# Second chunk of the first pass: Strassen's seven products in place of sixteen plain steps, with the weight sums made earlier

## Chip, core and metric

One core of one Trainium2 chip. The metric is the device time of one launch in microseconds (us), the median of several runs. The core has five engines with a queue of their own each, worked off in order: PE (TensorE, matmul), DVE (VectorE), ACT (ScalarE), POOL (GpSimd) and SP (SyncE, which here only issues DMAs). Engines wait for one another through semaphores. All data are float32.

## The reference

A retention block (attention with a decay mask and no softmax) feeds a two-layer network:

```python
# q, k, v: (8, 8, 576, 64)
scores = q @ k.T / sqrt(64)
ret    = (scores * Dmat) @ v          # Dmat[i, j] = gamma[h] ** (i - j) for i >= j, else 0
x = ret.transpose(0, 2, 1, 3).reshape(4608, 512)

# w_in: (512, 2048), w_out: (2048, 512)
h  = x @ w_in
sp = softplus(h)
g  = h * erf(sp)
out = g @ w_out                       # (4608, 512)
```

## The kernel before

**Pieces and stages.** The 8 x 576 tokens are cut into 36 pieces of 128 tokens (`pieces`). Each piece passes three stages (line 434): `transposes` (T), `scores` (S) and `outputs` (O). The text writes T8 for the transposition of piece 8, and so on. Pieces 0 to 7 have q and k transposed on PE and copied out of PSUM by ACT. From piece 8 on (`SQUARES`) q arrives in 32-column squares and is transposed on DVE (line 326), and from piece 12 on k too. S makes the score matrix on PE and multiplies it by the mask on DVE (`sT`, line 352). O multiplies by v on PE, scales the result into the token tile `x[0, c]` on DVE (two scalings, and between them a sum for the running state), multiplies the state by its decay on POOL (line 427) and emits loads for later pieces. `weigh_values` (line 313) multiplies the v of the next piece by its decay on POOL.

**Chunks and passes.** Four pieces are a chunk c of 512 tokens, so there are 9 chunks. The hidden width is cut into four groups g. A pass is one g over all chunks, and the tokens of chunk c are written to DRAM (`store_x`) in the first pass and read back (`load_x`) in the later ones. For every (g, c) there is a `First` (x times w_in, then softplus, erf, multiply) and a `Second` (times w_out). The text calls them F0, F1, F2 and S0, S1 for g = 0. S0 begins after F1.

**Strassen.** A `First` in the usual form makes seven products of 2 x 2 blocks in place of eight (`first`, `middle`, `last`). Their names are those of the weight operand: A11, A12, S2, S3, S1, S4, A22. Each is 4 matmuls, which the profile records as 8 of 128x256. They need sums of token blocks (`operands_x`, four DVE operations on 128x512 for g = 0) and sums of weight blocks (`sums_in`, four DVE operations, called "wa" in the list of a part's `sums`). `sums_in` overwrites the raw block A21 in the slot S3. The first two chunks of the first pass are `plain` instead: 16 steps of 2 matmuls (4 records) each, which read the raw blocks and the raw weights. `Second` has always seven products (B11, B21, T2, T3, T1, B22, T4) with the sums of `sums_out` ("wb").

**Weights.** They come as float64 words, and `rounding` turns them into float32. A part takes five steps: ACT (lines 254 and 255), DVE at 259, 263 and 267, and one step of DVE (272) with two POOL multiplications and additions (274 and 275; on DVE for the first four parts). `round_weights(n)` takes n steps. For g = 0 there are four parts of w_in and four of w_out.

**Order.** Nothing is scheduled by a planner: every engine works in the order in which the program emits. The start is a string of letters (line 754): `a` attends one stage, `p` is one plain step of F0, a digit is so many rounding steps, `w` loads weights. Then `attend(after_chunk(1))` brings the stages up to O7, and a loop over F1's plain steps puts one stage between every second of them, one rounding step after each, and F0's softplus, erf, multiply and sums at given steps. Then come S0's first two products, and the loop over `blocks` (line 789), in which each step of a product is followed by one stage through `attend`. Before F2 begins, all stages up to O11 are emitted and `operands_x(0, 2)` follows.

PSUM: F1 takes the banks `a` (two), `e` and `g`; stages take four banks `at`.

Of the kernel before, what the change touches and what calls it, by code (L numbers as in the profile page):

```python
# [2 lines left out]

# [1 line left out]

# [49 lines left out]
def kernel(  # L55
# [16 lines left out]
    n_dc = D_MODEL // P  # L72
    OH = D_MODEL // 2
    FH = D_FF // 2
    GP = 2
# [22 lines left out]
    def tt(out, in0, in1, op):  # L98
        nc.vector.tensor_tensor(out=out, in0=in0, in1=in1, op=op)  # L99
# [50 lines left out]
    def load(i, names="qkv"):  # L150
        if i < len(pieces):
            t = loaded.setdefault(i, {})
            for name in names:
                src = {"q": q, "k": k, "v": v}[name]
                if name == "q" and i < SQUARES:
                    t["q"] = load_rows(i, "q", q, 2)
                elif name == "q":
                    t["qs"] = load_squares(i, "q", q)
                    if i >= SQUARES_K:
                        t["ks"] = load_squares(i, "k", k)  # L160
                elif name == "v" or i < SQUARES_K or len(pieces[i]) == 1:
                    t[name] = load_rows(i, name, src, 4)
# [29 lines left out]
    def parts():  # L192

        w2 = w_in.rearrange("(e c d) (h f) -> c e d h f", c=n_dc, d=D, h=2)
        for g in range(n_g):
            for dc in range(n_dc):
                a = A11 if dc < 2 else A12
                src = [(heads[(e + dc) % 2], w2[dc, e, :, :, 2 * g * GW : 2 * (g + 1) * GW]) for e in range(2)]

                yield src, "wa", g, a, dc % 2, ["wa"] if g > 0 and dc == n_dc - 1 else []  # L200
            for f in range(2):
                for j in range(GP):
                    ft = f * FH // P + g * GP + j
                    src = [(slice(0, P), w_out[ft * P : (ft + 1) * P, :].rearrange("p (h o) -> p h o", h=2))]
                    sums = (["wb"] if g > 0 else ["wb", "wa"]) if (f, j) == (1, GP - 1) else []
                    yield src, "wb", g, B21 if f else B11, j, sums

    def sums_in(a11, s3, a12, a22, s1, s2, s4):
# [9 lines left out]
    def sums_out(b11, t3, b21, b22, t1, t2, t4):  # L218
# [7 lines left out]
        yield  # L226

    coming = parts()
    words = []
    most_g = [1]  # L230

    def load_weights():
        part = next(coming, None)
        if part is not None:
            t = wraw.tile([P, 2 * WP], UINT32, tag="wraw", name="wraw")
            for rows, src in part[0]:
                nc.sync.dma_start(out=t[rows].rearrange("p (h f) -> p h f", h=2), in_=src)
            words.append((t, *part[1:]))
# [49 lines left out]
    def round_weights(n=1):  # L288
        for _ in range(n):
            next(round_step, None)  # L290
# [149 lines left out]
    done = [0]  # L440

    def before_chunk(c):

        return stages.index((outputs, c * PC)) if c < n_ch else len(stages)

    def after_chunk(c):

        return stages.index((outputs, (c + 1) * PC - 1)) + 1

    def attend(upto):  # L450
        while done[0] < min(upto, len(stages)):
            of, i = stages[done[0]]
            of(i)
            done[0] += 1

    PLAIN = 2

    def load_x(g, c):  # L460
        x[g, c] = x_tile()
# [2 lines left out]
    def store_x(c):  # L464
        nc.sync.dma_start(out=xd[c], in_=x[0, c][:, :n_dc])
# [3 lines left out]
    def operands_x(g, c):  # L469
        summed.add((g, c))  # L470
        t = x[g, c]
        b11, b12, b21, b22 = (t[:, 2 * d : 2 * d + 2, h * TH : (h + 1) * TH] for d in range(2) for h in range(2))
        t1, t2, t4 = (t[:, n_dc + j, :].rearrange("p (d i) -> p d i", d=2) for j in range(3))
        if g == 0 or c < PLAIN:
            tt(t1, b12, b11, ALU.subtract)
            tt(t2, b22, t1, ALU.subtract)
            tt(b12, b22, b12, ALU.subtract)
        else:
            tt(t2, b12, b11, ALU.add)
            tt(t1, b22, t2, ALU.subtract)  # L480
        if g == 0:
            store_x(c)
        tt(t4, b21, t2, ALU.subtract)
        x[g, c] = {A11: b11, A12: b21, S4: b22, A22: t4, S1: t1, S2: t2, S3: b12}
# [240 lines left out]
    firsts = [First(g, c) for g, c in order]  # L725
    seconds = [Second(f) for f in firsts]
# [8 lines left out]
    def keep_busy(n):  # L735
        for _ in range(n):
            nc.tensor.matmul(idle[:, :P], lhsT=ones, rhs=ones, start=True, stop=True)


    most = [before_chunk(2)]  # L740

    def run(steps, rounds=(), stages=1):

        for step, _ in enumerate(steps):
            attend(min(done[0] + stages, most[0]))
            round_weights(rounds[step] if step < len(rounds) else 0)
# [4 lines left out]

    for what in "alkakakawkakakawwaa3awa2aaa5ppppaa5wwppa5ppawappwcppa5ppaaapp5s":
        if what == "a":
            attend(done[0] + 1)
        elif what == "p":
            next(products)
        elif what == "s":
            store_x(0)  # L760
        elif what == "l":
            load(2, "kv")
        elif what == "c":
            nc.sync.dma_start(out=cst[:, CONST_FIRST:], in_=consts[:, CONST_FIRST:])
        elif what == "w":
            load_weights()
        elif what == "k":
            keep_busy(2)
        else:
            round_weights(int(what))  # L770
    most[0] = before_chunk(3)
    attend(after_chunk(1))
    store_x(1)
    for step, _ in enumerate(firsts[1].plain()):
        if step % 2 == 0:
            attend(min(done[0] + 1, most[0]))
        round_weights(int(step > 1))
        if step == 1:
            firsts[0].softplus()
            firsts[0].erf()  # L780
        elif step == 5:
            firsts[0].multiply()
        elif step == 8:
            firsts[0].sums()
    seconds[0].begin()
    run(seconds[0].first(), (2, 2))
    firsts[1].softplus()
    most[0] = before_chunk(4)
    for b, nxt in zip(blocks[2:], blocks[3:] + [None]):
        n = order.index((b.g, b.c))  # L790
# [9 lines left out]
        elif n + 2 < n_s:  # L800
            f = firsts[n + 1]
# [62 lines left out]
```

## Time and profile before

| | |
|---|---|
| median of three runs | 1026.81 us (1025.83 to 1027.52) |
| the profiled execution, its own time | 1025.83 us |
| its span, first to last instruction | 1024.0 us |
| granted TensorE clock | 1.000 |
| PE, DVE, ACT, POOL busy in 50 to 75 us | 25.00, 15.87, 14.42, 9.14 of 25 us |
| PE, DVE, ACT, POOL busy in 75 to 100 us | 24.64, 23.20, 11.75, 8.66 of 25 us |
| PE, DVE, ACT, POOL busy in 100 to 125 us | 25.00, 21.12, 2.93, 3.87 of 25 us |
| F1's sixteen plain steps | from 59.72 us to 82.87 us, stages in between |
| F2's first product | 98.51 us |

All positions are microseconds from the start of the span. A line of a timeline gives start, duration, engine, line of the program, operation, output<-input, shapes and count, and in brackets how long the engine had been idle and who released it. Several equal instructions in a row are merged into one line. A matmul's duration includes the drain of the array, so the time that it takes from the next one is the distance of the starts.

### The profile page before, as it was taken

How to read it: one execution, taken by the hardware profiler on the slowest of the kernel's cores; microseconds unless marked ns; L12 is line 12 of the kernel's file. 1: busy time of each engine (PE TensorE's matmuls, PEld its weight loads, DVE VectorE, ACT ScalarE, POOL GpSimd, SP SyncE). 2: the span in 40 equal slices, each digit the busy share in tenths (PEclk: the TensorE clock that was granted, in tenths of full speed). 3: DMA queues.
4: the chain of work that ended last, by engine and by line, in shares of the span. 5: the costliest groups of instructions: out<-in, count | busy, mean ns of one | idle time of the engine just before them, and what ended most of it. 6: DMA issues, size and time to landing. Idle time of an engine off the chain costs nothing.

```text
span 1024.0 us, 15958 instructions
## 1 busy us (share of the span) xinstructions
PE 1017.6 (99%) x6348; PEld 876.0 (86%) x6348; DVE 667.6 (65%) x1062; ACT 390.2 (38%) x481; POOL 122.6 (12%) x122
## 2 busy tenths in 40 slices
PE   9999999999999999999999999999999999999998
PEld 8787888888888888888888888888888888888887
DVE  3769777976976656656666666666567655555555
ACT  3354134234134444334343444444433333333332
POOL 2143112122312110010001001000100000000000
PEclk9999999999999999999999999999999999999999
DMA  9998989979974354544444345444433333444434
GB/s 200 203 242 175 232 203 223 255 150 253 244 195 150 106 161 145 165 160 154 164 147 158 124 147 162 165 144 144 144 124 124 124 131 127 131 136 131 126 88 119
DMA packets 146986, 165.76 MB, mean 162 GB/s; under 512 B 97376, under 2 KB 121568, under 8 KB 138848
## 3 DMA queue, kind: packets, MB, share of 16 engines
q1 hardware_dynamic: 144832, 163.57, 56.4%
q10 hardware_dynamic: 2080, 1.18, 0.5%
q8 instruction: 50, 0.82, 0.4%
q14 instruction: 24, 0.20, 0.1%
HBM read 117.52 MB, written 47.19 MB: 161 GB/s over the span
## 4 chain that ended last, share of the span: by engine, by line
PE 94%; DMA 3%; DVE 2%; SPq 1%; POOL 1%; issue 0%; ACTq 0%; DVEq 0%; POOLq 0%
PE a L604 24%; PE a L496 23%; PE g L604 12%; PE g L496 12%; PE e L496 6%; PE e L604 6%; PE o L365 3%; PE s L347 3%; PE o L388 2%; DMA raw_k<-in_k_dram 1%; PE o L376 1%; DMA raw_v<-in_v_dram 1%; PE f L668 1%; SPq L147 1%; PE p L550 1%; PE h L668 1%
## 5 line engine op out<-in xcount | busy, mean ns | idle before, releaser
L496 PE MATMUL a<-x,wa 128*128 128x256 f32 x1088 | 258.3, 380 | 0.0
L496 PEld LDWEIGHTS a<-x,wa 128*128 128x128 f32 x1088 | 205.7, 190 | 28.5
L604 PE MATMUL a<-wb,s 128*128 128x256 f32 x840 | 200.0, 381 | 0.0
L604 PEld LDWEIGHTS a<-wb,s 128*128 128x128 f32 x840 | 158.4, 190 | 22.9 <-ACT o L618 0.7
L99 DVE TENSOR_TENSOR t<-g,t 128x512 f32<-128x512 f32 x68 | 47.0, 691 | 151.9 <-ACT t L526 114.1
L496 PE MATMUL g<-x,wa 128*128 128x256 f32 x544 | 129.2, 380 | 0.0
L496 PEld LDWEIGHTS g<-x,wa 128*128 128x128 f32 x544 | 102.8, 190 | 14.4
L99 DVE TENSOR_TENSOR o<-a,o 128x512 f32<-128x512 f32 x104 | 71.4, 687 | 46.4 <-PE a L604 46.4
L521 ACT COPY t<-a 128x512 f32<-128x512 f32 x34 | 19.9, 586 | 188.3 <-PE a L496 188.3
L99 DVE TENSOR_TENSOR t<-t,s 128x1024 f32<-128x1024 f32 x72 | 88.4, 1267 | 0.0
L274 POOL TENSOR_TENSOR wraw<-wraw 128x512 f32<-128x512 f32 x28 | 29.4, 1051 | 438.1 <-DVE wraw L272 184.4
L565 ACT ACTIVATE s<-t 128x1024 f32<-128x1024 f32 x72 | 72.1, 1049 | 24.6 <-DVE t L99 24.5
L99 DVE TENSOR_TENSOR x<-x 128x512 f32<-128x512 f32 x115 | 75.8, 693 | 1.2
L532 ACT COPY t<-a 128x512 f32<-128x512 f32 x34 | 19.9, 586 | 144.4 <-PE a L496 144.4
L569 ACT ACTIVATE s<-s 128x1024 f32<-128x1024 f32 x72 | 72.1, 1049 | 0.4
L604 PE MATMUL g<-wb,s 128*128 128x256 f32 x280 | 66.7, 381 | 0.0
L604 PE MATMUL e<-wb,t 128*128 128x256 f32 x280 | 66.6, 380 | 0.0
L604 PE MATMUL a<-wb,t 128*128 128x256 f32 x280 | 66.6, 380 | 0.0
L604 PE MATMUL g<-wb,t 128*128 128x256 f32 x280 | 66.4, 380 | 0.0
L99 DVE TENSOR_TENSOR sT<-s,cst 128x512 f32<-128x512 f32 x72 | 46.2, 682 | 30.4 <-PE s L347 30.4
L496 PE MATMUL e<-x,wa 128*128 128x256 f32 x272 | 64.8, 381 | 0.0
L99 DVE TENSOR_TENSOR o<-g,o 128x512 f32<-128x512 f32 x70 | 47.9, 684 | 20.9 <-ACT o L618 18.1
(86 smaller groups left out, 1247.1 us busy)
## 6 DMA issues: line engine op xcount, KB each, us to landing
od<-o SPq DMA_DIRECT2D x54, 512.0 KB, 3.3
x<-xd SPq DMA_DIRECT2D x27, 1024.0 KB, 4.8
o<-od SPq DMA_DIRECT2D x27, 1024.0 KB, 5.4
raw_qs<-in_q_dram SPq DMA_DIRECT2D x96, 112.0 KB, 4.4
raw_ks<-in_k_dram SPq DMA_DIRECT2D x84, 112.0 KB, 4.2
xd<-x SPq DMA_DIRECT2D x9, 1024.0 KB, 5.2
raw_v<-in_v_dram SPq DMA_DIRECT2D x64, 128.0 KB, 4.5
wraw<-in_moe_w_in_dram SPq DMA_DIRECT2D x32, 256.0 KB, 5.7
```

The lines of the kernel that those rows point to most:

```text
L99: nc.vector.tensor_tensor(out=out, in0=in0, in1=in1, op=op)
L274: engine.tensor_tensor(out=r_f, in0=high_f, in1=r_f, op=ALU.mult)
L347: nc.tensor.matmul(ps[e][:, p, :], lhsT=t["kT"][heads[e], p, :], rhs=t["qT"][heads[e], p, :], start=True, stop=True)
L365: nc.tensor.matmul(o[p % 2][heads[(e + p) % 2], p // 2, :], lhsT=t["v"][:, 2 * p + e, :], rhs=t["sT"][:, e, p, :], start=(p < 2), stop=(no ...
L388: nc.tensor.matmul(kv[heads[e], p, :], lhsT=t["k"][:, 2 * p + e, :], rhs=t["v"][:, 2 * p + e, :], start=False, stop=(p == NP - 1), skip_gr ...
L496: nc.tensor.matmul(acc[:, j * TH : (j + 1) * TH], lhsT=weights["wa", self.g][:, a, d, j * P : (j + 1) * P], rhs=x[self.g, self.c][a][:, d, :],
L521: nc.scalar.copy(out=self.t1[:, 1], in_=self.a)
L532: nc.scalar.copy(out=self.t2[:, 0], in_=self.a)
L565: nc.scalar.activation(self.s[:, j], t, AF.Softplus)
L569: nc.scalar.activation(self.s[:, j], self.s[:, j], AF.Erf)
L604: nc.tensor.matmul(acc[:, tp, :], lhsT=left[:, j * TH + tp * P : j * TH + (tp + 1) * P], rhs=weights["wb", self.g][:, b, j, :], start=(sta ...
L668: nc.tensor.matmul(acc, lhsT=left[:, j * TH + tp * P : j * TH + (tp + 1) * P], rhs=weights["wb", self.g][:, b, j, :], start=(b in (B11, B2 ...
```

## The change

F1 is made with the seven products. For this `PLAIN` goes from 2 to 1, which also makes `operands_x` of chunk 1 in the later passes use its three-operation branch. The four sums of the w_in blocks are emitted as soon as the four w_in parts are rounded (a `4` in the string between two plain steps of F0 and S6) and no more after the last part of w_out. `operands_x(0, 1)` follows O7, and `store_x(1)` is now issued inside it, after its third operation. The loop over F1 has 7 steps with one stage after each (7 stages, before 8), 14 rounding steps (before, 14 in the loop and 4 beside S0; the four that are gone are the moved sums), and F0's softplus and erf after the first product, its multiply after the third and its sums after the fifth. F1's softplus is now emitted within `last()`, ahead of S0's first two products, and not after them. No rounding is left beside S0.

```diff
-                yield src, "wa", g, a, dc % 2, ["wa"] if g > 0 and dc == n_dc - 1 else []
+                yield src, "wa", g, a, dc % 2, ["wa"] if dc == n_dc - 1 else []
...
-                    sums = (["wb"] if g > 0 else ["wb", "wa"]) if (f, j) == (1, GP - 1) else []
+                    sums = ["wb"] if (f, j) == (1, GP - 1) else []
...
-    PLAIN = 2
+    PLAIN = 1
...
-    for what in "alkakakawkakakawwaa3awa2aaa5ppppaa5wwppa5ppawappwcppa5ppaaapp5s":
+    for what in "alkakakawkakakawwaa3awa2aaa5ppppaa5wwppa5ppawappwcpp4a5ppaaapp5s":
...
     attend(after_chunk(1))
-    store_x(1)
-    for step, _ in enumerate(firsts[1].plain()):
-        if step % 2 == 0:
-            attend(min(done[0] + 1, most[0]))
-        round_weights(int(step > 1))
-        if step == 1:
+    operands_x(0, 1)
+    f = firsts[1]
+    for step, _ in enumerate(chain(f.first(), f.middle(), f.last())):
+        attend(min(done[0] + 1, most[0]))
+        round_weights((0, 2, 2, 2, 2, 3, 3)[step])
+        if step == 0:
             firsts[0].softplus()
             firsts[0].erf()
-        elif step == 5:
+        elif step == 2:
             firsts[0].multiply()
-        elif step == 8:
+        elif step == 4:
             firsts[0].sums()
     seconds[0].begin()
-    run(seconds[0].first(), (2, 2))
-    firsts[1].softplus()
+    run(seconds[0].first())
     most[0] = before_chunk(4)
```

More of the change, by code (lines that the diff above doesn't have):

```diff
@@ L2 @@
 from contextlib import ExitStack
+from itertools import chain
 import numpy as np
```

## The prediction

> **What bounds the kernel now.** I read the page's busy shares first, then the chain of waits, then the timelines of PE, DVE, ACT and POOL from 57 to 119 us.
>
> ```profile
> PE 1017.6 (99%) x6348; PEld 876.0 (86%) x6348; DVE 667.6 (65%) x1062; ACT 390.2 (38%) x481; POOL 122.6 (12%) x122
> ...
> PE 94%; DMA 3%; DVE 2%; SPq 1%; POOL 1%; issue 0%; ACTq 0%; DVEq 0%; POOLq 0%
> ```
>
> PE sets the end. In the chain from 100 us on there is nothing but PE, so whatever F2 starts earlier or later arrives at the end undiminished. Ahead of that the chain leaves PE once more, at about 64 to 87 us:
>
> ```profile
> 71.20 2.35 DVE t L99 x2
> 73.56 0.67 DVE x L99 x2
> ...
> 81.84 1.04 POOL wraw L274
> ...
> 82.97 1.62 POOL wb L275
> 84.61 1.51 DVE wb L99
> ```
>
> So in the stretch that the change rebuilds DVE is nearly as late as PE: 13.56 us busy of the 13.67 from 69.20 to 82.87. PE's own waits there are two: 0.27 before S10 (80.54 to 80.81) and about 0.52 in O10, whose first group took 1.61 instead of the usual 1.09:
>
> ```profile
> 80.81 1.16 PE L347 MATMUL s<-qT,kT 64*128 64x128 f32 x16 [0.27 <-DVE qT L326]
> ...
> 82.87 1.89 PE L604 MATMUL a<-wb,t 128*128 128x256 f32 x8
> 84.59 0.60 PE L332 MATMUL pt_k<-ident,raw_k 128*128 128x128 f32 x4
> 85.03 1.89 PE L604 MATMUL e<-wb,t 128*128 128x256 f32 x8
> 86.85 1.61 PE L365 MATMUL o<-sT,raw_v 128*64 128x128 f32 x16
> ```
>
> **Removed from PE.** The sixteen plain steps of F1 start 0.86 to 1.03 us before what follows them; these distances add up to 15.1 us. A product of 8 records takes 1.82 us (85.03 to 86.85) and 1.93 ahead of an S (89.60 to 91.53). F1 now has six of the one and one of the other: 12.85. Gain on PE: **-2.2 us**. With both old waits gone as well it would be -3.0, which is the most that this change can bring.
>
> **Weight sums moved to the front.** Four two-input DVE operations, 0.6 us apart (the four sums at 120.02 to 122.55), so 2.5 us. They are queued after O5's scaling, which ends at 46.1, and DVE then waits 3.45 us for S6's scores (49.54). They fit in; POOL's two operations there (45.90 and 46.47) may push them to 49.8, and S6's result is needed by O6 only at 52.23. Cost 0; without that gap it would be up to 2.5. What they write, S3, is read last by F0's plain steps before 41 us.
>
> **The new wait: the token sums stand ahead of T8 on DVE.** `operands_x(0, 1)` needs O7's last scaling (61.85), and behind it in DVE's queue are T8's transposes (two, 0.76 us together), for which S8 waits on PE. PE itself runs O7 to 59.72, A11 to 61.54, T8's k part to 61.98 and A12 to 63.80; A11 and A12 read raw blocks only. So S8 could start at 63.8. On DVE the four sums take 4 x 0.61 = 2.4 us if nothing disturbs them, and S8 starts at 61.77 + 2.4 + 0.75 + 0.15 = 65.1: **1.3 us** of waiting. But POOL is busy just then with four operations that are ready one after another: 1.04 (from 61.00), 1.28, 0.62, 1.05. What that does to two-input operations from SBUF is seen in chunk 2's `operands_x`:
>
> ```profile
> 99.48 0.88 DVE L99 TENSOR_TENSOR x<-x 128x512 f32<-128x512 f32 x1
> 99.77 1.49 POOL L313 TENSOR_TENSOR raw_v<-raw_v,cst 128x512 f32<-128x512 f32 x1
> 100.39 1.42 DVE L99 TENSOR_TENSOR x<-x 128x512 f32<-128x512 f32 x1
> 101.73 0.68 DVE L99 TENSOR_TENSOR x<-x 128x512 f32<-128x512 f32 x1
> ```
>
> They take turns: the first waits until POOL's operation before it ends (99.81) and then takes 0.55; POOL's next one, 0.45 longer than its usual 1.04, ends at 101.26; the second DVE operation ends 0.55 later. Put on 61.77 us: first sum done 62.6, POOL 1.28 to 63.75, second 64.3, POOL 0.62 to 64.8, third 65.3, POOL 1.05 to 66.2, fourth 66.8, transposes to 67.45, S8 at 67.6: **3.8 us** of waiting. I take this end, since the same operations with the same neighbours showed it in five places (also the 1.51 above), and keep 1.3 as the other.
>
> One rule of the Trainium skill speaks against so long a wait. TensorE: Matmul & The Clock Gate, section "What's actually happening", says that a window of about 3.4 us without work halves TensorE's clock. No row of this profile shows it, since the granted clock is 1.00 in every stretch and no wait of PE here is above 1.1 us. By that page the sum would be about 1.7 us higher, if a free-running window fell wholly into the wait; this is an estimate from the page and is in no number below.
>
> **ACT.** F0's softplus and erf come after A11's copy and T8's copy, so the block that began at 61.38 begins at 62.25; rounding's line 254 behind it moves from 68.50 to 69.37, and DVE's line 259, which before too stood waiting for it (3.69 us idle), from 69.21 to 70.08. Behind it in DVE's queue are T9's transposes, F0's multiply and all that follows.
>
> **DVE from there to O10.** Before, this row of work ran from 69.21 to 87.3. In it now are additions of 0.6 each for the second half of F1's products S1 and A22 (1.2) and the last two sums of `sums_out` ahead of S10's masking (1.2; before, after it). F0's sums no longer meet POOL (-1.0, the 1.77 at 76.00). And the addition after S1 must wait for that product: PE, after S8 at 67.6, does S8, S2, T9, S3, O8 (1.09, 1.82, 0.44, 1.82, 1.65) to 74.4 and S1 to 76.35, ACT copies until 77.1, so DVE stands about 1.3 us. After it: S9's masking to 78.95, F0's sums to 82.3, T10 and rounding to 84.5, A22's addition and O9 to 86.1, POOL's last weights at 86.8 (0.65 waiting), the first remaining sum to 88.3 (1.5, as before, beside POOL's v), two more, S10's masking to **90.7**.
>
> PE meanwhile: S9, S4, T10, A22, O9, B11, S10, B21, T11 end at 88.25 without a wait. T2 starts at 88.4 (its weight sum) and O10 at 90.2; half of S10's result is 0.45 late. New waits: 3.8 + 0.15 + 0.45 = 4.4; old ones gone, -0.8; work, -2.2. Sum **+1.4 us**: F2's first product at 99.9 in place of 98.51.
>
> **What is late next.** The loop attends 7 stages and not 8, so T12 (DVE 0.63 + 0.98) no longer stands after T3 but with O11 after T1, just ahead of `operands_x(0, 2)`. By the sum above S12's masking ends at 106.4 and O12 needs it at 106.6: 0 cost, but with only 0.2 of slack (before, 1.0).
>
> **SP and the DMAs.** `store_x(1)` waits for the third sum (65.3), and SP comes to it only at 67.88: 0. The loads behind T9's and T10's transposes are freed about 1.5 and 2.3 us later; T12's data, issued by about 87.5 then and 2.9 to 4.4 in landing, are used at 99: 0. Later passes save three DVE operations of 0.69 us, which PE's end doesn't see: 0. F1's softplus, now ahead of B11's copy on ACT, lets that copy end at 87.75; T2 needs the bank at 88.25: 0, and 0.6 if DVE's addition were that much later.
>
> **Against the measured time.** The profiled execution took 1025.83 with a span of 1024.0. The span becomes 1025.4, the time 1027.2. The median shown is 0.98 above the profiled execution, so on its scale **1028.2**.
>
> **Rivals.**
> - *The sums go undisturbed.* S8 then starts at 65.1, 2.5 us earlier, but DVE is still held by ACT until 70.08 and reaches the end of S10's masking at 88.9 instead of 90.7, so only 1.7 of it arrives: 1026.81 - 0.3 = **1026.5**. For it: POOL may be late. Against: line 274 started at 61.00 with its input from a step that the change leaves alone.
> - *PE's work is all that counts*: -3.0, **1023.8**. It needs T8 ready at 63.8, so four sums and T8 in 2 us; 128x512 sums at 0.6 don't allow it, unless DVE's work before is earlier. Its weaker forms, with small waits, reach to 1024.8.
> - *Slower: T12's place.* DVE goes into chunk 2 too late. T1's addition, T12 (1.6), O11's three scalings and four contended sums follow one another, and O12 waits. It decides from the moment when S12's masking ends after 106.6. Price up to the 1.6 us of T12's two transposes: +1.4 + 1.6 = +3.0, **1029.8**. For it: 0.2 us of slack in a row of some twenty durations. Against: DVE then has no rounding left, which before cost it 5 us from 87.2 to 94.4 (six sums).
> - *The change not doing what it says*: the plain line 550 would keep its 128 records (F0's and F1's) and not fall to 64; the diff calls the three parts of the product form, so nothing speaks for it.
>
> **How the numbers follow.** I put 0.2% (2.05 us) as what a measurement of this kernel tells from no change. That is below 1024.8 and above 1028.9. Forecast 0.44, its own range 1027.3 to 1029.4, of which 0.28 lies within the bound and 0.16 above it; undisturbed sums 0.20 (within); T12 0.24 (slower); PE alone 0.12 (faster). So faster 0.12, within 0.48, slower 0.40. The range for 8 in 10 goes from the weak form of the fast case, 1024.9, to 1030.6, which is the price of T12 with 0.8 more for a longer wait of S8.
>
> **What would show it.** Right: S8 starts near 67.6 with over 3 us idle before it, released by DVE's T8 transposes, and `operands_x` lasts about 5 us from 61.8; line 259 at about 70.1 behind ACT; F2's first product near 99.9. Wrong: S8 before 65.5; a granted clock under 1 after the wait; O10 without a wait; O12 idle for more than 0.5; any wait before 57 us from the early weight sums; a chain after 110 us with other engines than PE.

## The result and the profile after

The changed kernel took 1032.3 us in the median of 4 runs (1030.61 to 1033.54), against 1026.97 before (1025.83 to 1027.52): the ratio is 1.0052, with an interval of 1.0035 to 1.0070. Run again on another chip it was 1031.64 (5 runs) against 1027.69 (20 runs), 1.0038 (1.0024 to 1.0052). So it is slower by 4 to 5 us; the forecast was 1028.2, with a range to 1030.6. The clock, averaged over the span, was 0.996 to 0.998 in all nine executions of the changed kernel, and 0.999 or 1.000 in the twenty of the kernel before on that other chip.

In the kernel before S8 had nothing to wait for, since T8's transposes on DVE were made ahead of it:

```profile
61.77 0.76 DVE L326 STREAM_TRANSPOSE qT<-raw_qs 128x256 f32<-128x256 f32 x2
...
63.03 1.16 PE L347 MATMUL s<-qT,kT 64*128 64x128 f32 x16
```

PE's timeline from A11 to T9 in the kernel after (columns as before; line 99 of the kernel before is line 100 here, and from line 200 on the numbers are the same):

```profile
60.78 1.99 PE L496 MATMUL a<-x,wa 128*128 128x256 f32 x8
62.61 0.60 PE L332 MATMUL pt_k<-ident,raw_k 128*128 128x128 f32 x4
63.05 1.89 PE L496 MATMUL e<-x,wa 128*128 128x256 f32 x8
68.62 1.16 PE L347 MATMUL s<-qT,kT 64*128 64x128 f32 x16 [3.69 <-DVE qT L326]
69.72 3.48 PE L496 MATMUL a<-x,wa 128*128 128x256 f32 x8
72.99 0.84 PE L332 MATMUL pt_k<-ident,raw_k 128*128 128x128 f32 x4
```

S8 waits for T8's transposes as forecast. But the product behind it, S2, takes 3.27 us to the start of T9 instead of 1.82. The view by stretches of the same kernel shows a lower clock there (stretch, its length, PE, PEld, DVE, ACT, POOL busy, granted clock, DMA share, GB/s):

```profile
64.00:68.00 4.00, 0.94 (x5) 0.48 (x3) 4.00 (x4) 3.97 (x4) 4.00 (x4) 1.00 1.18 335
68.00:72.00 4.00, 3.38 (x22) 2.88 (x23) 3.23 (x7) 3.64 (x5) 0.70 (x1) 0.76 1.17 319
72.00:76.00 4.00, 4.00 (x25) 3.12 (x26) 3.43 (x5) 2.33 (x4) 0.00 (x0) 0.82 1.07 271
```

In steps of one microsecond the clock is 0.50 from about 70.1 to 73.5. It fell after PE had come back to work at 68.62, so useful matmuls ran at the lower clock. That this is what made S2 long is tested below (PE kept warm).

Why S8 waits so long is seen on DVE and POOL in the kernel after:

```profile
62.94 4.85 DVE L100 TENSOR_TENSOR x<-x 128x512 f32<-128x512 f32 x4
67.72 0.76 DVE L326 STREAM_TRANSPOSE qT<-raw_qs 128x256 f32<-128x256 f32 x2
...
63.17 1.61 POOL L275 TENSOR_TENSOR wb<-wb,wraw 128x512 f32<-128x512 f32 x1
64.75 1.05 POOL L427 TENSOR_TENSOR state<-sums,cst 128x256 f32<-128x256 f32 x1
65.77 2.93 POOL L313 TENSOR_TENSOR raw_v<-raw_v,cst 128x512 f32<-128x512 f32 x2
```

Four sums that were put at 2.4 us undisturbed last 4.85, and POOL's operations are lengthened too (1.61 for 1.28, 1.05 for 0.62).

Landmarks split the difference of the two spans, 7.0 us. "O7" is O7's first matmul, "F2" F2's first product, "O17" and "O35" the first state products of the pieces 17 and 35:

| profile | O7 at | O7 to F2 | F2 to O17 | O17 to O35 | O35 to end |
|---|---|---|---|---|---|
| before | 57.48 | 41.03 | 131.23 | 83.22 | 711.04 |
| before, second profile | 57.98 | 41.04 | 131.23 | 83.22 | 711.03 |
| after | 58.54 | 44.40 | 131.23 | 85.71 | 711.12 |
| after, second profile | 58.63 | 45.51 | 131.23 | 85.03 | 711.10 |

O7's own position is not counted as the change's: it lies between 57.48 and 59.66 us in the profiles of this document, and the two profiles of the kernel before alone differ by 0.5. From O7 to F2 the change costs 3.4 and 4.5 us. Nearly all of the rest is at O17 to O35, where PE waits for DVE's transposed k and DVE for its load. These are DVE's waits for loads from 110 to 340 us in the kernel after (engine, operation, what it waited for: us in total, times, longest):

```profile
DVE kT L326 <- DMA raw_ks<-in_k_dram: 6.1, 6, 1.8
...
DVE qT L326 <- DMA raw_qs<-in_q_dram: 3.2, 3, 2.3
```

Before, these were 1.2 and 0.7 us in the first profile, but 3.7 and 2.1 in the second, without a wait of PE. One thing upstream stands out in the kernel after: SP stood 7.8 us before the loads for piece 12 (from 77.7 to 85.65), since their buffer was T10's and DVE came to T10 at 84.92; in that hole the DMA engines moved 3 GB/s from 80 to 85 us. Before, the same loads were issued at 80.69.

### The profile page after: what moved, and what is told of

Its sections match the earlier page's. It is cut to its first block, busy times and chain, and to the rows that moved or that the text cites. A ratio compares the mean times of both kernels' runs of the same rounds, so it can differ in the third digit from the quotient of the medians.

```text
span 1031.0 us, 15944 instructions
## 1 busy us (share of the span) xinstructions
PE 1018.2 (99%) x6340; PEld 875.7 (85%) x6340; DVE 672.1 (65%) x1066; ACT 390.4 (38%) x481; POOL 124.5 (12%) x122
## 4 chain that ended last, share of the span: by engine, by line
PE 89%; DMA 6%; DVE 2%; SPq 2%; issue 0%; POOL 0%; ACTq 0%; DVEq 0%; POOLq 0%
PE a L604 23%; PE a L496 23%; PE g L496 12%; PE g L604 11%; PE e L604 6%; PE e L496 5%; PE s L347 3%; PE o L365 3%; DMA raw_ks<-in_k_dram 2%; DMA raw_v<-in_v_dram 2%; PE o L388 1%; PE o L376 1%; SPq L148 1%; DMA raw_k<-in_k_dram 1%; PE f L668 1%; SPq L132 1%
## 5 line engine op out<-in xcount | busy, mean ns | idle before, releaser
L496 PE MATMUL a<-x,wa 128*128 128x256 f32 x1120 | 267.7, 382 | 0.0
L496 PEld LDWEIGHTS a<-x,wa 128*128 128x128 f32 x1120 | 212.3, 191 | 29.9
L496 PE MATMUL g<-x,wa 128*128 128x256 f32 x560 | 133.0, 380 | 0.0
L496 PEld LDWEIGHTS g<-x,wa 128*128 128x128 f32 x560 | 105.7, 190 | 14.7
L100 DVE TENSOR_TENSOR x<-x 128x512 f32<-128x512 f32 x116 | 78.8, 712 | 1.3
```

The source lines that it names most:

```text
L496: nc.tensor.matmul(acc[:, j * TH : (j + 1) * TH], lhsT=weights["wa", self.g][:, a, d, j * P : (j + 1) * P], rhs=x[self.g, self.c][a][:, d, :],
```

## The experiments

In this section the kernel before, in times and ratios, is always that run on the same chip as the experiment.

**T8 ahead of the sums.**

```diff
+    attend(done[0] + 1)
     operands_x(0, 1)
     f = firsts[1]
     for step, _ in enumerate(chain(f.first(), f.middle(), f.last())):
-        attend(min(done[0] + 1, most[0]))
+        if step > 0:
+            attend(min(done[0] + 1, most[0]))
```

> The changed kernel with T8 emitted ahead of the token sums of chunk 1 (and no stage after A11, so that the rest of the order stays). If S8's wait behind the four sums (3.69 us in the changed kernel's profile) and the half clock that follows it (S2 3.27 instead of 1.82 us) are the loss: S8 starts within 0.5 us of A12's end, the clock stays at 1.00, S2 waits at most 1 us for its own sum, and the time falls by 4 to 5 us, to about 1027.5. If the four contended sums only move the wait from S8 to S2 with the same length: time within 1 us of the changed kernel's 1032.3.

Measured: 1028.33 (10 runs) against 1027.92 (28), ratio 1.0007 (0.9998 to 1.0016). S8 didn't wait, S2 waited 0.18, the clock stayed at 1.00, O7 to F2 took 41.59. So the order of T8 and the sums carries nearly the whole loss. There was no gain either; PE's timeline of this kernel shows where it went:

```profile
83.73 1.13 PE L604 MATMUL e<-wb,t 128*128 128x256 f32 x4
86.44 1.13 PE L604 MATMUL e<-wb,t 128*128 128x256 f32 x4 [1.58 <-POOL wb L275]
```

B21's second half waited 1.58 us for the last w_out part, which POOL finishes late; that DVE and ACT come late to its rounding is what the reordered kernel below tests.

**PE kept warm.**

```diff
         if step == 1:
+            warm = ps_e.tile([P, W], FP32, tag="g", name="warm")
+            for _ in range(12):
+                nc.tensor.matmul(warm[:, :P], lhsT=ones, rhs=ones, start=True, stop=True)
         attend(min(done[0] + 1, most[0]))
```

> The changed kernel with twelve small matmuls on constants between A12 and S8, in the time in which PE waits anyway; nothing else is altered. If the idle PE lost its clock and this is a cost of its own: granted clock 1.00 from 64 to 76 us, S2 takes 1.82 us, S8 starts where it did (3.8 us after A12's end), and the time is 1.5 to 1.9 us below the changed kernel's. If the longer S2 is from something else (operands late, PSUM): S2 still takes over 3 us and the time doesn't fall.

Measured: 1030.37 (7 runs), 1.0024 (1.0013 to 1.0035). In this kernel the stretches read:

```profile
64.00:68.00 4.00, 4.00 (x31) 3.69 (x29) 3.97 (x4) 3.96 (x5) 4.00 (x4) 1.00 1.13 340
68.00:72.00 4.00, 2.98 (x26) 2.60 (x26) 3.23 (x8) 3.99 (x5) 1.13 (x1) 1.00 1.18 343
72.00:76.00 4.00, 4.00 (x62) 3.28 (x61) 3.86 (x5) 2.31 (x5) 0.00 (x0) 1.00 0.97 221
```

S2 took 1.83 (70.15 to 71.98), S8 still came 3.9 us after A12's end, and O7 to F2 took 42.73: 1.67 less than the kernel after. That is the price of the fallen clock by itself (1.45 in S2 and 0.24 in T9, read in the profile after), and 1.70 is what remains of the waits less the saved work.

**Only the early weight sums.** The kernel before with the `4` in the string and the sums out of the w_out part; F1 stays plain. Its plain steps then read the slot S3 after the sums have overwritten it, so its hidden values of chunk 1 are not the reference's; the work and its order are.

> The kernel before with only the four weight sums moved to the front (F1 stays plain). If they are hidden in DVE's wait ahead of S6, as the forecast said, and relieve DVE later: no wait of PE before 60 us that wasn't there, O10's wait of 0.5 us goes or shrinks, time 0 to 0.8 us below the kernel before. If the early sums cost something of their own (they meet POOL at 46 us): 0.5 to 2 us above it.

Measured: 1027.72 (10 runs), 0.9998 (0.9988 to 1.0007); O7 to F2 41.02. Hidden, as forecast. They relieve nothing.

**SP held in the kernel before.** `load(12, ...)` is taken out of T10 and O9 and follows a store of 8 columns of S0's first result.

```diff
...
-    run(seconds[0].first(), (2, 2))
+    hold = dram.tile([P, 8], FP32, tag="hold", name="hold", bufs=1)
+    for step, _ in enumerate(seconds[0].first()):
+        if step == 0:
+            nc.sync.dma_start(out=hold, in_=seconds[0].o[:, 0, 0, :8])
+            load(12, "q")
+            load(12, "kv")
+        attend(min(done[0] + 1, most[0]))
+        round_weights(2)
```

> The kernel before with SP held, as it is in the changed kernel: the loads for piece 12 come only after a small store of S0's first result (about 85.4 us instead of 80.7), PE, DVE and ACT keep their order. If the hole in the transfers at 80 to 85 us is what makes k and q late at 230 to 280 us: the time rises by 1.5 to 3 us, with PE waiting for transposed k between 200 and 300 us. If those late loads are chance or come from elsewhere: within 0.7 us of the kernel before.

Measured: 1029.71 (10 runs, 1027.43 to 1032.67), 1.0022 (1.0009 to 1.0034). O7 to F2 is 41.04 as before, so nothing changed on PE up to there, and yet 1.8 us are lost by the medians: holding these loads (issued at 86.50 and not at 80.69) does cost time. Where it is lost isn't shown, because the profiled execution is the fastest of the ten (1027.43, below the median of the kernel before). Its waits of DVE for k and q after 100 us, 5.2 and 4.3 us, are no sign of the loss: with the early weight sums alone, which lose nothing, they are 5.8 and 3.5.

**The changed kernel again, and the one before.**

> The changed kernel as it is, on the same chip as the three runs beside it. If three losses add up (about 1.7 us from O7 to F2 by waits less the work saved, 1.7 by the halved clock, 1.5 to 2 by late loads): 4.5 to 5.5 us above the kernel before, F2's first product 44.0 to 44.8 us after O7's first matmul (before: 41.03), the clock under 1.00 once, at S2. If the late loads were chance: 3 to 4 us above.

> The kernel before, for a second profile of it. If late loads between 230 and 315 us are the price of SP's hole at 80 to 85 us: O17 to O35 (the last pieces with a small state product) takes 83.2 to 84.0 us, as in the first profile (83.2), against 85.7 in the changed kernel. If they are chance: anything from 83 to 86.

The changed kernel was 1.0038 above (some 4 us), with 45.51 from O7 to F2: the clock was at 0.50 for 6.8 us this time (67.7 to 74.6, by steps of one microsecond), so S8 ran slow too. The time is that of the second theory (late loads by chance), but O7 to F2 is above what either said. The second profile of the kernel before repeats 83.22 from O17 to O35. But that row is not a clean measure: with the early sums alone it was 85.12, without any loss of time in the median. The profiled executions of the kernel before (1025.83 and 1026.34) are near its fastest; its median on the other chips is 1027.7 to 1028.4.

**POOL kept quiet during the sums.**

```diff
-    "...wcpp4a5ppaaapp5s"
+    "...wcpp4a5ppaaapp4s"
...
-        if i + 1 >= SQUARES:
+        if i + 1 > SQUARES:
             weigh_values(i + 1)
...
     operands_x(0, 1)
+    round_weights(1)
+    weigh_values(SQUARES)
```

> The changed kernel with POOL kept quiet while DVE makes the token sums of chunk 1: the last rounding step of the second w_out part (one DVE and two POOL operations) and the weighing of piece 8's v are emitted after the four sums; only O7's state operation (0.62) stays. If taking turns with POOL made the sums long: they last 2.5 to 3.2 us instead of 4.85, S8 waits 1.3 to 2.2 us instead of 3.69, the clock stays at 1.00, and the time falls by 2.5 to 4 us against the changed kernel. If the sums are slow for another reason: 4.85 and 3.69 stay, and so does the time.

Measured: 1029.09 (10 runs), 1.0009 (1.0000 to 1.0018); O7 to F2 41.69. From this kernel's timelines of PE and DVE:

```profile
66.20 1.16 PE L347 MATMUL s<-qT,kT 64*128 64x128 f32 x16 [1.51 <-DVE qT L326]
...
62.23 2.80 DVE L100 TENSOR_TENSOR x<-x 128x512 f32<-128x512 f32 x4
```

2.80 instead of 4.85, and a wait of 1.51 instead of 3.69, with the clock at 1.00 (over the span 1.000 in all ten executions): taking turns with POOL is what made the wait long.

**Reordered.** T8 first, and besides: two rounding steps ahead of F0's softplus, half of F0's sums and two of the w_out sums beside S0's first products (`rounded` is then marked after the second sum, since B11 and B21 don't need the sums).

```diff
-        round_weights((0, 2, 2, 2, 2, 3, 3)[step])
+        round_weights((2, 2, 2, 2, 2, 1, 1)[step])
...
-            firsts[0].sums()
+            firsts[0].sums((0,))
...
-    run(seconds[0].first())
+    for step, _ in enumerate(seconds[0].first()):
+        attend(min(done[0] + 1, most[0]))
+        if step == 0:
+            firsts[0].sums((1,))
+        round_weights()
```

> T8 ahead of the token sums, as in the run with T8 first, and besides: two rounding steps ahead of F0's softplus on ACT, two sums of F0 and two of the w_out blocks moved beside S0's first two products. If what kept the run with T8 first from a gain was rounding standing behind softplus and erf on ACT and DVE's full queue (B21 waited 1.58 us for POOL's last weights): that wait goes, F2's first product comes 38.5 to 39.5 us after O7's first matmul (41.03 before, 41.59 with T8 first), and the time is 1 to 2.5 us below the kernel before. If DVE's sum of work is the bound whatever its order: F2 at 41 or later and no gain.

Measured: 1027.84 (10 runs), 1.0000 (0.9990 to 1.0009); O7 to F2 40.52. B21's wait is gone, but neither theory came true: F2 is earlier than before by 0.5 us and not by 1.5 to 2.5, and the time is the same. S3 waited 1.07 us for DVE, whose operations meet POOL again (F0's multiply 3.20, a weight step 1.15).

**Reordered, with POOL quiet.** Both edits together, and the rounding steps as `(2, 2, 0, 2, 2, 2, 2)`, F0's first sums one step later.

> The reordered kernel with POOL kept quiet during the token sums (as in the run with POOL quiet), the third w_out part's weights on POOL after F0's multiply instead of beside it, and F0's sums after T10. If the remaining waits of the reordered kernel (S3 1.07, S2 0.22, T2 0.25 us) come from DVE operations lengthened by POOL (multiply 3.2 instead of 2.35, sums 1.4 instead of 0.6): F2's first product 38.8 to 39.8 us after O7's first matmul (40.52 in the reordered kernel, 41.03 before), time 1 to 2 us below the kernel before. If a gain ahead of F2 is eaten by loads that come no earlier: F2 as early, but the time within 0.7 us of the kernel before, and PE waits for transposed k between 230 and 315 us.

Measured: 1025.8 (6 runs) against 1028.39 (11): 0.9975 (0.9964 to 0.9986). O7 to F2 takes 38.69. PE's waits from 58 to 98 us in this kernel (us in total, times, longest), all that the view of waits lists:

```profile
PE a L496 <- ACT t L521: 0.4, 1, 0.4
```

So with next to no waiting the stretch is 2.3 us shorter than before (the kernel before's own two waits, 0.8 us, are in that difference), and 2.6 us arrive at the end (1.4 to 3.7 by the interval). This version is faster than the kernel before. Late loads it has all the same: the loads for piece 12 were issued at 78.52, and O17 to O35 still took 84.41, with one wait of PE of 0.82 us for transposed k.

**PE warm, with a shorter hole.** The run with PE kept warm, with F0's sums at `step == 5`, after T10.

> The run with PE kept warm, with F0's sums emitted after T10 and not before it, so that DVE transposes T10 some 2.5 us earlier and SP's hole after 78 us is that much shorter; O10 waits for the same sum of DVE work. If the hole costs time by late loads: 0.7 to 1.5 us below the run with PE kept warm (2.45 us above the kernel before), so 1 to 1.7 above before. If it doesn't: 2 to 3 above before.

Measured: 1032.8 (5 runs), 1.0043 (1.0029 to 1.0056): neither theory. SP issued the loads for piece 12 at 81.31 instead of 84.40, and O17 to O35 fell from 84.56 to 83.63. But F0's sums now stood beside POOL's last weights (1.53, 1.66 and 1.53 us each instead of 0.6), A22's addition and F1's softplus came later, and T2 waited 1.52 us for its bank:

```profile
91.27 2.95 PE L604 MATMUL a<-wb,s 128*128 128x256 f32 x8 [1.52 <-ACT o L618]
94.15 1.77 PE L365 MATMUL o<-sT,raw_v 128*64 128x128 f32 x16
```

T2 then took 2.88 us to the next start, because the clock fell here too: in steps of one microsecond it is 0.50 from about 92.2 to 95.6. Over the span it was 0.998 in three of the five executions and 1.000 in two, so the same kernel lost its clock in some and kept it in others. O7 to F2 took 45.83. The edit brought a wait and a slow stretch of its own, so it doesn't settle what the hole costs the changed kernel.

**Four warming matmuls instead of twelve.**

> The changed kernel with four small matmuls after A12 instead of twelve, so that PE's wait before S8 is about 2.8 us instead of 3.69 (and 1.51 with POOL quiet, where the clock held). If a wait has to fill about 3.4 us for the clock to fall: 1.00 throughout. If any long wait does it: the clock falls to 0.5 for about 3.4 us, S2 takes over 3 us.

Measured in one profiled execution: S8 waited 2.80 us, and still the clock fell to 0.50, from about 70.0 to 73.4 us. Stretches of this kernel:

```profile
68.00:72.00 4.00, 2.24 (x17) 2.05 (x18) 2.54 (x5) 3.97 (x5) 1.83 (x2) 0.75 1.17 328
72.00:76.00 4.00, 4.00 (x18) 3.41 (x18) 3.96 (x8) 2.26 (x5) 0.00 (x0) 0.83 1.04 329
```

S8 and S2 took 1.85 and 2.69 us, O7 to F2 44.34. So the wait need not fill 3.4 us; 2.80 was enough. Nor does its length alone decide: 1.52 us were enough in the profile of the run with the shorter hole, while 1.51 (POOL quiet), 1.58 (T8 first) and 1.02 (PE kept warm) were not. What else decides isn't shown.

## Why the prediction was wrong

**The new wait** was right in place, cause and size. S8 waits on T8, which stands behind the sums, which take turns with POOL: 3.8 us forecast, 3.69 measured; from O7's first matmul S8 was put at 10.1 us and came at 10.08. Without the turns the forecast was 1.3, and the run with POOL quiet has 1.51.

**Waits less work** were put at +1.4; the run with PE kept warm, whose clock stayed at 1.00, shows +1.70. The order of the sum held, down to the wait in O10 (0.45 forecast; its first group took 1.50 instead of 1.09) and T12, whose move cost nothing: S12's masking ended at 109.39 and O12 followed without a wait at 109.61. The one rival that led to a slower kernel was thus the wrong one.

**The step that failed first is the clock.** It was weighed only by a page's rule, priced at 1.7, tied to a window that would have to fall wholly into the wait, and kept out of every number; a clock under 1 after the wait stood in the prediction only as a sign of being wrong. It came in both profiles of the changed kernel, and cost 1.7 (first profile; shown by the run with PE kept warm) and about 2.8 in the second (45.51 less 42.73). TensorE: Matmul & The Clock Gate of the Trainium skill, section "What's actually happening", gives the half clock rightly, and about 3.4 us or more of work until the clock is full again (first profile: 3.4; second: 6.8, twice that). Its condition of an idle window of about 3.4 us does not agree with the waits of 2.80 and 1.52 us that sufficed here; so the price of 1.7 met the first profile although the condition it was tied to did not hold.

**The second is "SP and the DMAs: 0".** That step asked only whether the next use of piece 12 was late. It did not ask whether a hole in the loads can be made up later; in the kernel before the DMA share is 0.75 to 1.1 until 300 us. The held SP shows 1.8 us (0.9 to 3.5 by the interval of the ratio) for such a hole in the kernel before. How much of it the changed kernel pays is open: its two results, 5.3 and 4.0 us above, less the 3.4 and 4.5 from O7 to F2 of one profile each, leave between +1.9 and -0.5. O17 to O35 doesn't settle it either: it was 83.2 us in both profiles of the kernel before, but 85.12 and 84.41 in two kernels that issued these loads at 81.22 and 78.52 (early weight sums alone; reordered with POOL quiet).

**Hidden, as forecast**: the early weight sums (0.9998) and the store of chunk 1 (67.83 instead of 67.88). The rival of undisturbed sums was put at -0.3; the run with POOL quiet came out 1.4 us above by the medians (1.0009, 1.0000 to 1.0018), with 0.8 us of B21 waiting for POOL's weights, which the sum hadn't.

## What to carry to other kernels

An operation put ahead of a stage in a shared queue should be asked what stands behind it: here four additions delayed two short transposes, on which PE depended, and swapping the two orders took away nearly all of the loss. A PE wait can cost more than its length: after about 3 us of it the clock halved in every profile here, and after about 1.5 us in one of three, so a wait of that size has to be priced with a slow stretch after it, or filled. Work saved on the bounding engine arrives only if the engines that feed it keep up: the same seven products gave +4 to +5, about 0 and -2.6 us, by the order of DVE's, ACT's and POOL's work.

## What was not expected of the hardware

- The clock fell to 0.50 after waits of 3.69 and 2.80 us of PE, and once after 1.52, but not after 1.51 and 1.58. In the changed kernel's first profile it fell 1.5 us after PE had resumed (68.62 and 70.1), and in its second while PE still waited (67.7); it stayed there for 3.4 and 6.8 us.
- DVE and POOL took turns, operation by operation, when both read two inputs from SBUF: 4.85 us for four additions that took 2.58 with POOL quiet (in the last reordered version). A one-input weight step was lengthened as well (0.43 to 1.15 us beside POOL's weighing of v, reordered version).
- Holding the loads for piece 12 by some 5 us cost the kernel before 1.8 us (0.9 to 3.5), although nothing changed on PE up to F2; no profile shows where.
